# An H3 and feed-forward kernel: the convolution's f16 parts go into the signal's own place, weight factors are joined, and an output buffer is taken from a second ring

## The chip, the cores and the metric

The kernel runs on one core of a Trainium2 chip. The metric is the device time in microseconds (us) of one execution; lower is better. Engine names are those of the profile: PE (TensorE matmul), PEld (its weight load), DVE (VectorE), ACT (ScalarE), POOL (GpSimd, which here only issues adding DMAs), SP (SyncE, which issues all other DMAs).

## What is computed

With S = 2048 rows, D = 1024 channels and F = 3584 hidden features, all f32:

```python
xn = layernorm(q)
h3 = xn * (causal_conv(kv, ssm_k) + kv * ssm_D)      # kv = short_conv(k, 4 taps) * v, per channel
ff = silu(xn @ w1) @ w2
out = q + h3 + ff
```

The long convolution has 2048 taps for each of the 1024 channels. In the reference it goes by FFT.

## The kernel before, in words

**Feed-forward.** Both matrix products run in f16 with each operand split in a high and a low part, so that one logical product is three matmuls (hi*hi, hi*lo, lo*hi; lines 958 to 960 for w1, 1101 to 1103 for w2). Most of it goes by a Strassen scheme with seven products, P1 to P7, whose weight operands are called B11, T2, T3, B21, B22, T1 and T4. `factors_w1` (line 762) builds them from each pair of w1 columns on DVE (sums) and ACT plus DVE (`split`: ACT writes the high part, DVE the low one). They live in the ring `wo` (six tiles of two halves) and are also stored to DRAM (`ws`) and loaded again for the second half of the rows. Before the change T1 is a difference in a tile of its own (`t1`), split by itself, and T4 is another.

A unit is one set of seven products into PSUM banks `ff`. `evacuate` (first product) and `evacuate2` (line 1185, second product) copy banks out. In `evacuate2` the values of P6 and P5 go to `a` and `d`, P1+P2 and P3 are taken by `copied`; all of these are halves of the ring `hf` (three tiles, six halves), and each is then added to `out` by a DMA that POOL issues. In the last unit only, `copied` may take a half of the ring `ht` (two tiles, four halves) instead, and the old output that `a` needs is loaded to an `ht` half. PE may start P3 of a unit when ACT has read P5 out of the bank that they share (line 1167).

**Convolution.** It runs in 8 groups of 128 channels beside the feed-forward. For a group: `gate` (line 1468) squares the filter `kf` on ACT for its scale, makes kv in `acc` from `kin` (one ACT copy and three DVE multiply-adds for each half b of the rows) and multiplies by v in quarters. `signal_parts` (line 1519) splits `acc` by t in f16 parts: group 0 is transposed by PE first; for the others the parts go to `cm` and are transposed by DMA into tiles of the rings `hi` and `lo` (two tiles each), one tile holding signal and filter for one t. `stage1` (line 1553) multiplies them with a constant DFT matrix; `to_spec`, `forward`, `product` and `inverse` (DVE butterflies on the tile `spec`, in place) follow, then `result_parts`, `stage1_inv` and `gated`, which writes or adds to `out`. The rings `hi` and `lo` also serve as place for the quarters of v and for the outputs of the squares.

**Order.** Nothing is ordered by hand. Generators yield operations with a modelled duration and a bias, and at build time a planner (`Order.run`, line 262) picks the next one by modelled start time less bias. Each engine then runs its instructions in that order, and each DMA queue issues in that order, with semaphores between engines. Where a generator yields `ring.ready`, that is a question to the planner; the wait on the chip is on the last readers of the buffer that it got. An edit that changes a duration or a buffer can so change the order of everything planned after it.

Of the kernel before, what the change touches and what calls it, by code (L numbers as in the profile page):

```python
# [20 lines left out]
P = 128  # L21
# [40 lines left out]
FACTORS = (("B11",), ("T2", "T3"), ("B21", "B22"), ("T1",), ("T4",))  # L62
# [238 lines left out]
def h3_ffn_kernel(ctx, tc, x, kp, vs, fs, shift, dskip, w1, w2, cfwd, cinv, out):  # L301
# [132 lines left out]
    t1_r = Ring(order, rawa, "t1", 1)  # L434
# [326 lines left out]

    def factors_w1():
        for n, (kind, i) in enumerate(pairs):
# [421 lines left out]
    def evacuate2(u, one, made, seen):  # L1185

        last = u == len(tiles2) - 1

        def copied(src, tok, to):
            yield lambda: hfs.ready() or last and hts.ready()  # L1190
            o, otok = (hts if last and hts.ready() else hfs).tile([P, W])
# [22 lines left out]
        yield ws_r.ready  # L1214
        d, dt = ws_r.tile([P, W])
# [193 lines left out]
    TO = (1, 3, 0, 2)  # L1409

    def convolution(floor):
# [5 lines left out]
        def ring(name, bufs, pool=ra):  # L1417
            return Ring(order, pool, name, bufs)

        kin_r, kf_r, acc_r, hi_r, lo_r = (ring(*a) for a in (  # L1420
            ("kin", 1), ("kf", 1), ("acc", 1), ("hi", 2), ("lo", 2)))
# [5 lines left out]
        kins, kfs, accs, scs, sss, part, ipart, xgs, tmps, vals = ({} for _ in range(10))  # L1427
# [15 lines left out]
        def loads():  # L1443
            for g in range(NG):
                for b in range(2):
                    yield kin_r.ready
                    kins[g, b] = kin, _ = kin_r.tile([P, T2 + HALO, P])
                    yield L(kin, kp[g, b])
                    flag["kin", g, b].set()
                    if b == 0:  # L1450
                        yield kf_r.ready
                        kfs[g] = kf, _ = kf_r.tile([P, 2, T2, P], uses=4)
                        yield L(kf, fs[g])
                        yield G(kf[0:1, 0, 0, :], dskip[g:g + 1, :])
                        flag["kf", g].set()

        def load_v():

            for g in range(NG):
                yield flag["acc", g]  # L1460
                for b in range(2):
                    for q in range(2):
                        yield lambda: hi_r.ready() or lo_r.ready()
                        vals[g, b, q] = v, _ = (hi_r if hi_r.ready() else lo_r).tile([P, TQ, P])
                        yield L(v, vs[g, b][:, q * TQ:(q + 1) * TQ])
                        flag["v", g, b, q].set()

        def gate():

            for g in range(NG):  # L1470
# [6 lines left out]
                yield acc_r.ready  # L1477
                accs[g] = acc, _ = acc_r.tile([P, 2, T2, P])
# [6 lines left out]
                flag["acc", g].set()  # L1485
                tap = [taps[:, g, j:j + 1] for j in range(TAPS)]
                for b in range(2):
# [19 lines left out]
                yield from norm_on_two(py_r, ss[:, 0:6], (4, 2), scales, [flag["scales", g]], 4.0)  # L1507
# [3 lines left out]
        def parts_tile(hr, lr, shape=(P, 2, 2, 2, P)):  # L1511
# [7 lines left out]
        def signal_parts():  # L1519

            for g in range(NG):
                yield flag["scales", g]
                acc, atok = accs[g]
                kf, ktok = kfs[g]
                sc, _ = scs[g]
                for t in TO:
                    if g < BY_DMA:
# [8 lines left out]
                        (hi, htok), (lo, ltok) = part[g, t] = yield from parts_tile(hi_r, lo_r)  # L1536
                        flag["part", g, t].n = 2
                        add(split(hi[:, 0], lo[:, 0], px, sc[:, 0:1], (ptok, flag["part", g, t])), CB)
                        add(split(hi[:, 1], lo[:, 1], kf[:, :, t::4, :], sc[:, 1:2], (ktok, flag["part", g, t])), CB)
# [4 lines left out]
                    (hi, htok), (lo, ltok) = part[g, t] = yield from parts_tile(hi_r, lo_r)  # L1544
                    flag["part", g, t].n = 3
                    add(split(hi[:, 1], lo[:, 1], kf[:, :, t::4, :], sc[:, 1:2], (ktok, flag["part", g, t])), CB)
# [4 lines left out]
                atok.set()  # L1551

        def stage1():

            for g in range(NG):
# [3 lines left out]
                tmps[g] = tmp, _ = tmp_r.tile([P, 2, 2, 2, 2 * P])  # L1559
                for t in TO:  # L1560
                    yield flag["part", g, t]
                    (hi, htok), (lo, ltok) = part.pop((g, t))
                    two = []
                    for i in range(2):
                        for c in range(2):
                            if i == 0:
# [3 lines left out]
                                diff = (tmp[:, :, t // 2] if t % 2 else sp[:, :, 4 + t])[:, :, c]  # L1570
                                add(to_spec(g, t, sp[:, :, t, c, :], diff, *two[c], tok), CB)
# [4 lines left out]
                            def mm():  # L1576
# [3 lines left out]
                                h, l = hi[:, :, :, i], lo[:, :, :, i]  # L1580
# [3 lines left out]
                            yield T(mm, ps, [hi, lo], 0.65, m=3.0 if g > 0 and t == TO[0] else 1.0)  # L1584
                            (made if i else two[c][3]).set()
                    htok.set()
                    ltok.set()
# [17 lines left out]
        def forward(g):  # L1605
# [3 lines left out]
            def C(a, n=1, step=1):  # L1609
                t, a = (tmp, a - 8) if a >= 8 else (sp, a)  # L1610
                return t[:, :, a:a + (n - 1) * step + 1:step, :, :]

            def R(a):
                return C(a)[:, :, 0, 0, :]

            def I(a):
                return C(a)[:, :, 0, 1, :]

            def R2(a, step):
                return C(a, 2, step)[:, :, :, 0, :]  # L1620

            def I2(a, step):
                return C(a, 2, step)[:, :, :, 1, :]

            yield flag["spec", g, 1]
            yield v_tt(R2(5, 2), R2(8, 1), I2(8, 1), ADD)
            yield v_tt(I2(5, 2), I2(8, 1), R2(8, 1), SUB)
# [3 lines left out]
            yield v_tt(C(5, 2, 2), C(0, 2), C(2, 2), SUB)  # L1631
            yield v_tt(C(2, 2), C(0, 2), C(2, 2), ADD)
# [57 lines left out]
        def inverse(g):  # L1690


            def C(a, n=1, step=1):
                h, a = a // 8, a % 8
                return sp[:, h, a:a + (n - 1) * step + 1:step, :, :]

            def R(a):
                return C(a)[:, 0, 0, :]

            def I(a):  # L1700
                return C(a)[:, 0, 1, :]

            yield v_tt(C(8, 4, 2), C(0, 4, 2), C(1, 4, 2), ADD)
# [219 lines left out]
```

## Time and profile before

| | |
|---|---|
| median of 3 runs | 1249.17 us (1248.23 to 1249.23) |
| the profiled execution | 1247.09 us, span of its instructions 1245.0 us |
| granted TensorE clock | 1.00 |
| busy PE / DVE / ACT / POOL | 1232.0 / 1118.5 / 788.4 / 83.6 us |
| DMA | 279.84 MB, mean 225 GB/s |

The profile's times are microseconds from the first instruction. Busy time of an engine is the time in which at least one of its instructions was in flight; a releaser is what ended an idle stretch.

### The profile page before, as it was taken

How to read it: one execution, taken by the hardware profiler on the slowest of the kernel's cores; microseconds unless marked ns; L12 is line 12 of the kernel's file. 1: busy time of each engine (PE TensorE's matmuls, PEld its weight loads, DVE VectorE, ACT ScalarE, POOL GpSimd, SP SyncE). 2: the span in 40 equal slices, each digit the busy share in tenths (PEclk: the TensorE clock that was granted, in tenths of full speed). 3: DMA queues.
4: the chain of work that ended last, by engine and by line, in shares of the span. 5: the costliest groups of instructions: out<-in, count | busy, mean ns of one | idle time of the engine just before them, and what ended most of it. 6: DMA issues, size and time to landing. Idle time of an engine off the chain costs nothing. (4 is left out here: it accounts for less than half of the span.)

```text
span 1245.0 us, 17285 instructions
## 1 busy us (share of the span) xinstructions
PE 1232.0 (99%) x6092; PEld 601.9 (48%) x6092; DVE 1118.5 (90%) x1360; ACT 788.4 (63%) x1431; POOL 83.6 (7%) x93
## 2 busy tenths in 40 slices
PE   9999999999999999999999999999999999999997
PEld 8544444444444544444444544544544444454453
DVE  7999996996999789999999799899999889997981
ACT  7778888876688878669563823753453464554252
POOL 0000000000000000000000000000120030123223
PEclk9999999999999999999999999999999999999999
DMA  9376998879799899859984665579496498978757
GB/s 368 102 263 233 321 302 296 287 233 200 227 327 286 247 294 338 225 168 281 354 304 131 172 214 135 168 263 258 106 225 178 117 195 237 256 142 154 157 121 103
DMA packets 272807, 279.84 MB, mean 225 GB/s; under 512 B 73808, under 2 KB 192848, under 8 KB 271440
## 3 DMA queue, kind: packets, MB, share of 16 engines
q1 hardware_dynamic: 256992, 262.22, 68.2%
q0 software_dynamic: 15728, 16.52, 10.0%
q8 instruction: 47, 0.77, 0.2%
q14 instruction: 40, 0.33, 0.1%
HBM read 175.66 MB, written 88.34 MB: 212 GB/s over the span
## 5 line engine op out<-in xcount | busy, mean ns | idle before, releaser
L1101 PE MATMUL ff<-x,wo 128*128 128x512 f16 x868 | 328.1, 378 | 2.8 <-ACT hf L360 2.2
L1103 PE MATMUL ff<-x,wo 128*128 128x512 f16 x868 | 328.1, 378 | 0.0
L1102 PE MATMUL ff<-x,wo 128*128 128x512 f16 x868 | 328.1, 378 | 0.0
L958 PE MATMUL ff<-x,wo 128*128 128x512 f16 (+1 forms) x808 | 302.8, 375 | 1.3 <-DVE hf L349 0.9
L960 PE MATMUL ff<-x,wo 128*128 128x512 f16 (+1 forms) x808 | 302.8, 375 | 0.0
L959 PE MATMUL ff<-x,wo 128*128 128x512 f16 (+1 forms) x808 | 302.8, 375 | 0.0
L349 DVE TENSOR_TENSOR spec<-spec 128x512 f32<-128x512 f32 (+2 forms) x256 | 261.5, 1052 | 2.1
L1102 PEld LDWEIGHTS <-wo 128*128 128x128 f16 x868 | 84.9, 98 | 101.9 <-issue 3.3
L1103 PEld LDWEIGHTS <-wo 128*128 128x128 f16 x868 | 84.9, 98 | 101.6
L1101 PEld LDWEIGHTS <-wo 128*128 128x128 f16 x868 | 85.8, 99 | 98.8
L960 PEld LDWEIGHTS <-wo 128*128 128x128 f16 x808 | 79.0, 98 | 92.1
L958 PEld LDWEIGHTS <-wo 128*128 128x128 f16 x808 | 80.4, 100 | 87.9
L959 PEld LDWEIGHTS <-wo 128*128 128x128 f16 x808 | 79.0, 98 | 89.8 <-issue 1.9
L349 DVE TENSOR_TENSOR tmp<-spec 128x2048 f32<-128x2048 f32 (+1 forms) x48 | 92.7, 1933 | 0.9
L352 DVE SCALAR_TENSOR_TENSOR ht<-hf,wsc,ht 128x1024 f16<-128x1024 f32 (+1 forms) x56 | 67.3, 1203 | 7.0 <-ACT ht L360 5.3
L360 ACT ACTIVATE ht<-hf,wsc 128x1024 f16<-128x1024 f32 (+1 forms) x56 | 60.8, 1085 | 8.5 <-DMA hs<-ht 3.5
L352 DVE SCALAR_TENSOR_TENSOR wo<-raw,wsc,wo 128x512 f16<-128x512 f32 (+1 forms) x56 | 56.5, 1013 | 7.3 <-ACT wo L360 6.9
L360 ACT ACTIVATE spec<-spec 128x1024 bf16<-128x1024 f32 x32 | 33.7, 1054 | 45.6 <-DVE spec L349 45.6
L352 DVE SCALAR_TENSOR_TENSOR acc<-kin,taps,acc 128x1024 f32<-128x1024 f32 x48 | 61.4, 1279 | 0.6 <-ACT acc L360 0.5
L349 DVE TENSOR_TENSOR spec<-tmp 128x512 f32<-128x512 f32 (+1 forms) x80 | 60.9, 793 | 0.9
L346 POOL DMA_DIRECT2D kf<-in_dskip x8 | 7.4, 922 | 801.8 <-DMA kf<-in_fs 327.2
L346 POOL DMA_DIRECT2D out<-hf x45 | 40.7, 911 | 298.5 <-ACT hf L360 201.8
(193 smaller groups left out, 1798.7 us busy)
## 6 DMA issues: line engine op xcount, KB each, us to landing
wo<-hs SPq DMA_DIRECT2D x160, 256.0 KB, 3.5
hs<-ht SPq DMA_DIRECT2D x80, 256.0 KB, 4.3
raw<-in_w SPq DMA_DIRECT2D x28, 512.0 KB, 5.8
wraw<-in_w SPq DMA_DIRECT2D x24, 512.0 KB, 5.8
w2n<-in_w SPq DMA_DIRECT2D x24, 512.0 KB, 5.9
out<-hf POOLq DMA_DIRECT2D x45, 256.0 KB, 4.3
kin<-in_kp SPq DMA_DIRECT2D x16, 704.0 KB, 5.1
xt<-in_x SPq DMA_DIRECT2D x16, 512.0 KB, 7.4
```

Of the source, the lines that this page charges most:

```text
L346: return Op("POOL", 1.1, 3.0, lambda: nc.gpsimd.dma_start(o, i, accum_op=ADD), [i], [o], m, 2.3 * n)
L349: return V(lambda: nc.vector.tensor_tensor(o, a, b, op=op), o, [a, b], **k)
L352: return V(lambda: nc.vector.scalar_tensor_tensor(o, a, s, b, op0=op0, op1=op1), o, [a, b] + ([] if isinstance(s, float) else [s]), **k)
L360: nc.scalar.activation(o, i, func, scale=scale, **kw)
L958: nc.tensor.matmul(o, w[:, 0, k], xf[:, :, k, 0], start=first and k == 0, stop=False, **kw)
L959: nc.tensor.matmul(o, w[:, 0, k], xf[:, :, k, 1], start=False, stop=False, **kw)
L960: nc.tensor.matmul(o, w[:, 1, k], xf[:, :, k, 0], start=False, stop=last and k == KH - 1, **kw)
L1101: nc.tensor.matmul(po, hx[:, n, 0, :], wc[:, n, 0, :], start=first and n == 0, stop=False, **kw)
L1102: nc.tensor.matmul(po, hx[:, n, 0, :], wc[:, n, 1, :], start=False, stop=False, **kw)
L1103: nc.tensor.matmul(po, hx[:, n, 1, :], wc[:, n, 0, :], start=False, stop=last and n == 3, **kw)
```

## The change

Three groups of edits. **w1 factors:** T4 and T1 become one double factor: `B21|B22 - T2`, with T2 read twice by a step of 0, and one split of 1024 elements a partition for both; the tile `t1` goes, and the two are stored and loaded together. **Convolution:** `acc` and a second half of the same size become one tile `sig`; v is loaded whole for each b to the second half and multiplied in one product; the filter's f16 parts are then written to that second half in one split over the whole `kf`, and the signal's f16 parts go back to the place of `acc`, also by the transposing DMAs; `hi` and `lo` go. A group's `gate` and its loads of v now wait until `stage1` of the group before has read both. `stage1` waits for all of the filter's parts once. The butterflies get another slot order in `spec` (`AT`), by which more of them can be joined: 4 scaled additions become 2 in `forward`, and `inverse` has 13 instead of 16 instructions over the same elements. **Last unit:** `d` in `evacuate2` may take a half of `ht`, as `copied` already may.

The parts of the diff that carry this:

```diff
-FACTORS = (("B11",), ("T2", "T3"), ("B21", "B22"), ("T1",), ("T4",))
+FACTORS = (("B11",), ("T2", "T3"), ("B21", "B22"), ("T4", "T1"))
...
             yield from part(("B11",), b[0, 0])
-            yield t1_r.ready
-            t1, t1k = t1_r.tile([P, KH, P])
-            yield v_tt(t1, b[0, 1], b[0, 0], SUB)
             yield v_tt(b[0, 1], b[1, 1], b[0, 1], SUB)
             yield v_tt(b[0, 0], b[0, 1], b[0, 0], ADD)
             yield from part(("T2", "T3"), hv[0])
             yield from part(("B21", "B22"), hv[1])
-            yield from part(("T1",), t1)
-            t1k.set()
-            yield v_tt(b[1, 0], b[1, 0], b[0, 0], SUB)
+            two = hv[1].rearrange("p k (f w) -> p k f w", f=2)
+            yield v_tt(two, two, again(b[0, 0]), SUB)
             toks[0].set()
-            yield from part(("T4",), b[1, 0])
+            yield from part(("T4", "T1"), hv[1])
...
+        def place():
+            yield lambda: hfs.ready() or last and hts.ready()
+            return (hts if last and hts.ready() else hfs).tile([P, W])
...
-        yield ws_r.ready
-        d, dt = ws_r.tile([P, W])
+        d, dt = yield from place()
         yield made["P5"]
         yield a_act(d, two, AF.Copy, invc2[:, 0:1])
...
+    AT = (0, 2, 3, 1, 4, 6, 5, 7)
...
+        sig = ra.tile([P, 2, 2, T2, P], F32, name="sig")
+        acc = sig[:, 0]
+        acc16 = acc.bitcast(F16)
+        kparts = sig[:, 1].bitcast(F16).rearrange("p b t w -> p b (t w)").rearrange("p b (q t w) -> p b q t w", q=2, t=T2)
...
+        def signal(t2, q):
+            return pair(acc16[:, :, t2, q * P:(q + 1) * P], kparts[:, :, q, t2, :])
...
             for g in range(NG):
-                yield flag["acc", g]
+                if g > 0:
+                    yield flag["stage1", g - 1]
                 for b in range(2):
-                    for q in range(2):
-                        yield lambda: hi_r.ready() or lo_r.ready()
-                        vals[g, b, q] = v, _ = (hi_r if hi_r.ready() else lo_r).tile([P, TQ, P])
-                        yield L(v, vs[g, b][:, q * TQ:(q + 1) * TQ])
-                        flag["v", g, b, q].set()
+                    yield L(sig[:, 1, b], vs[g, b])
+                    flag["v", g, b].set()
...
+                if g > 0:
+                    yield flag["stage1", g - 1]
                 for a in range(2):
-                    yield hi_r.ready
-                    j, tok = hi_r.tile([P, T2, P], BF16)
-                    yield a_act(j, kf[:, a], AF.Square, total=ss[:, 4 + a:5 + a])
-                    tok.set()
+                    j = acc[:, a].bitcast(BF16)[:, 0:TQ].rearrange("p t w -> p (t w)")
+                    yield a_act(j, kf[:, a].rearrange("p t w -> p (t w)"), AF.Square, total=ss[:, 2 + a:3 + a])
...
-                    for q in range(2):
-                        yield flag["v", g, b, q]
-                        v, tok = vals.pop((g, b, q))
-                        o = acc[:, b, q * TQ:(q + 1) * TQ]
-                        yield v_tt(o, o, v, MUL)
-                        yield a_act(v, o, AF.Square, total=ss[:, 2 * b + q:2 * b + q + 1])
-                        tok.set()
+                    yield flag["v", g, b]
+                    v = sig[:, 1, b]
+                    yield v_tt(o, o, v, MUL)
+                    yield a_act(v, o, AF.Square, total=ss[:, b:b + 1])
...
+                whole = [kparts[:, :, q].rearrange("p b t w -> p b (t w)") for q in range(2)]
+                add(split(*whole, kf.rearrange("p b t w -> p b (t w)"), sc[:, 1:2], (ktok, flag["kparts", g])), CB)
                 for t in TO:
+                    there = acc16.rearrange("p b (i t) w -> p (b i) t w", i=2)[:, :, t]
+                    two = [there[:, :, q * P:(q + 1) * P] for q in range(2)]
...
-                    add(split(hi[:, 1], lo[:, 1], kf[:, :, t::4, :], sc[:, 1:2], (ktok, flag["part", g, t])), CB)
-                    for q, o in enumerate((hi, lo)):
-                        yield X(o[:, 0].rearrange("p b i w -> p (b i) w"), cm[:, q].rearrange("p b i w -> p (b i w)"))
+                    flag["part", g, t].n = 2
+                    for q, o in enumerate(two):
+                        yield X(o, cm[:, q].rearrange("p b i w -> p (b i w)"))
...
+                yield flag["kparts", g]
                 for t in TO:
                     yield flag["part", g, t]
-                    (hi, htok), (lo, ltok) = part.pop((g, t))
...
-                                h, l = hi[:, :, :, i], lo[:, :, :, i]
+                                h, l = (signal(t + 4 * i, q) for q in range(2))
...
+                flag["stage1", g].set()
...
-            for o, s, t, r in ((4, 8, 5, -RT), (5, 8, 5, RT), (6, 9, 7, -RT), (7, 9, 7, RT)):
-                flat = [C(a)[:, :, 0].rearrange("p s c w -> p s (c w)") for a in (o, s, t)]
-                yield v_stt(flat[0], flat[1], r, flat[2], MUL, ADD)
+            yield v_stt(long(sp[:, :, 4:6]), long(tmp), -RT, long(sp[:, :, 6:8]), MUL, ADD)
+            yield v_stt(long(sp[:, :, 6:8]), long(tmp), RT, long(sp[:, :, 6:8]), MUL, ADD)
```

More of the change, by code (lines that the diff above doesn't have):

```diff
@@ L1187, in evacuate2 @@
         last = u == len(tiles2) - 1
+        def place():
+            yield lambda: hfs.ready() or last and hts.ready()
+            return (hts if last and hts.ready() else hfs).tile([P, W])
         def copied(src, tok, to):
-            yield lambda: hfs.ready() or last and hts.ready()
-            o, otok = (hts if last and hts.ready() else hfs).tile([P, W])
+            o, otok = yield from place()
             yield a_act(o, src, AF.Copy, invc2[:, 0:1])
@@ L1426, in convolution @@
         ctxs["nm"] = py_r
-        kins, kfs, accs, scs, sss, part, ipart, xgs, tmps, vals = ({} for _ in range(10))
+        kins, kfs, scs, sss, ipart, xgs, tmps = ({} for _ in range(7))
         more = {}
@@ L1690, in inverse, with C @@
         def inverse(g):
[L1693 to L1695 removed]
+            def C(a, b=None):
+                one = sp[:, a // 8, AT[a % 8]].rearrange("p c w -> p (c w)")
+                return one if b is None else pair(one, C(b))
             def R(a):
[L1698 removed]
+                return C(a)[:, 0:2 * P]
             def I(a):
[L1701 removed]
@@ L1739, in result_parts @@
                     (hi, htok), (lo, ltok) = ipart[g, t] = yield from parts_tile(more["zh"], more["zl"], (P, 2, 2 * 2 * P))
-                    yield from split(hi, lo, sp[:, 1, t::4].rearrange("p i c w -> p i (c w)"), sc[:, 4:5],
+                    two = pair(sp[:, 1, AT[t]], sp[:, 1, AT[4 + t]]).rearrange("p i c w -> p i (c w)")
+                    yield from split(hi, lo, two, sc[:, 4:5],
                                      (flag["taken", g, t], flag["ipart", g, t]))
```

93 lines of the change are left out of this document (40 added, 53 removed).

## The prediction

> **What bounds the kernel now.** I read the page first, then one long window of the table of windows, then PE's timeline at each of its gaps.
>
> ```profile
> span 1245.0 us, 17285 instructions
> PE 1232.0 (99%) x6092; PEld 601.9 (48%) x6092; DVE 1118.5 (90%) x1360; ACT 788.4 (63%) x1431; POOL 83.6 (7%) x93
> 15.72:1232.30 1216.58, 1212.71 (x5956) 585.17 (x5954) 1105.92 (x1324) 776.94 (x1406) 80.26 (x84) 1.00 0.79 225
> ```
>
> PE is busy for 1232.0 of 1245.0 us. The third line is the stretch from the first feed-forward matmul to the gap near the end: PE is busy for 1212.71 of 1216.58 us, so only 3.87 us are idle there. Is a busy PE also full? Consecutive 128x512 matmuls tell:
>
> ```profile
> 1230.87 0.38 PE L1101 MATMUL ff<-x,wo 128*128 128x512 f16 x1
> 1231.09 0.38 PE L1102 MATMUL ff<-x,wo 128*128 128x512 f16 x1
> 1231.31 0.38 PE L1103 MATMUL ff<-x,wo 128*128 128x512 f16 x1
> ...
> 1231.95 0.38 PE L1103 MATMUL ff<-x,wo 128*128 128x512 f16 x1
> ```
>
> They last 0.38 us each but start 0.216 us apart (1.08 us from the first to the fourth shown, five steps with the two left out), one hiding behind the other. How many of that shape there are:
>
> ```profile
> L1101 PE MATMUL ff<-x,wo 128*128 128x512 f16 x860 | 325.9, 379 | 2.2 <-ACT hf L360 2.2
> L958 PE MATMUL ff<-x,wo 128*128 128x512 f16 x776 | 294.0, 379 | 1.3 <-DVE hf L349 0.9 <-ACT x L360 0.5
> L1581 PE MATMUL ps<-hi,cfw 128*128 128x512 f16 x108 | 40.9, 379 | 0.6 <-ACT tmp L360 0.6
> ```
>
> Three lines each of the first two kinds, and stage 1 with 384 in the source (8 groups, 4 values of t, 2 x 2 x 3; 108 of the 128 of a line go to `ps`, the others to `ff`): 3 x 860 + 3 x 776 + 384 = 5,292, times 0.216 = 1,143 us. The rest of 1232 is taken by shapes of half that width, transposes and warm-up. So PE is at its pace nearly throughout. The Trainium skill ("Perfetto Trace Analysis", Identifying the Most-Contended Engine) says that matmul busy time is a bad measure of headroom and names the share of weight loads instead; that share is 48% here and by it half the time could still be won. The start times above decide otherwise: the busy time holds no hidden slack.
>
> The change leaves every matmul and its size as it is, except small sums for norms (4 columns in place of 6). So DVE, ACT and DMA can move the time only through PE's gaps. These are the ones after the start phase:
>
> ```profile
> 42.44 1.82 PE L598 MATMUL ft<-ident,xt 128*128 128x128 f32 x12 [0.34 <-DVE x L352]
> 45.43 0.63 PE L598 MATMUL ft<-ident,xt 128*128 128x128 f32 x4 [1.17 <-DVE x L352]
> 204.01 0.38 PE L958 MATMUL ff<-x,wo 128*128 128x512 f16 x1 [0.46 <-ACT x L360]
> 323.88 0.38 PE L958 MATMUL ff<-x,wo 128*128 128x512 f16 x1 [0.87 <-DVE hf L349]
> 430.52 0.38 PE L1581 MATMUL ps<-hi,cfw 128*128 128x512 f16 x1 [0.60 <-ACT tmp L360]
> 782.88 0.27 PE L1773 MATMUL py<-zl,civ 128*128 128x256 f16 x1 [0.41 <-DVE zl L352]
> 1234.56 0.38 PE L1101 MATMUL ff<-x,wo 128*128 128x512 f16 x1 [2.23 <-ACT hf L360]
> ```
>
> The first six sum to 3.85 us, which is the idle time of the long window. The last, 2.23 us, is the only large one, and it stands where nothing can make it up.
>
> **The gap at 1232.3 us.** ACT, POOL and SP there:
>
> ```profile
> 1216.77 3.34 POOL L346 DMA_DIRECT2D out<-ht  x3 [0.55 <-issue]
> 1217.29 0.33 SPq L336 DMA_DIRECT2D ht<-out  x1
> 1222.60 2.22 POOL L346 DMA_DIRECT2D out<-ht  x2 [2.50 <-issue]
> 1224.60 0.69 ACT L360 ACTIVATE hf<-ff,invc 128x512 f32<-128x512 f32 x1 [4.49 <-PE ff L1103]
> 1227.61 1.78 POOL L346 DMA_DIRECT2D out<-hf  x2 [2.79 <-issue]
> 1228.24 5.48 DMA out<-hf
> 1233.83 0.69 ACT L360 ACTIVATE hf<-ff,invc 128x512 f32<-128x512 f32 x1 [8.54 <-DMA out<-hf]
> ```
>
> This is the last unit: P6 is copied at 1224.60 into `a`, P5 at 1233.83 into `d`. A product is 12 matmuls, 2.59 us, so P7 and P5 follow to about 1229.8 and P2 to 1232.3. `d` could thus have been copied at 1229.8. But its `hf` half was still being added to `out` by a DMA that POOL issued at 1228.24 (behind the convolution's last `out<-ht` additions) and that landed at 1233.72. P3 waits for `d`, hence 2.23 us of idle PE.
>
> **The change part by part.** (1) *Last unit.* `d` may now be a half of `ht`. The load of the old output takes one half, at 1217.29; a second half of the same tile is picked first. It last held a result of the convolution whose addition was issued in the `out<-ht` batches of 1216.77 or, at worst, 1222.60 to 1224.82. Landing in the 5.48 us of the row above, that is about 1225 or, at worst, 1230.3; with the copy's 0.69 us `d` is read by 1231.0, before P2 ends at 1232.3. So the whole 2.23 us goes: what is late next is P2 itself, which is PE's own work. The rest of the tail moves as one: P3, two halves of P4, one DVE addition and the last stores. Gain 2.2 us; bounds 0 (no half of `ht` is free for the planner) and 2.23.
>
> (2) *w1 factors.* Fourteen pairs, with rows
>
> ```profile
> L352 DVE SCALAR_TENSOR_TENSOR wo<-raw,wsc,wo 128x1024 f16<-128x1024 f32 x28 | 35.7, 1278 | 4.3 <-ACT wo L360 4.1
> L360 ACT ACTIVATE wo<-raw,wsc 128x1024 f16<-128x1024 f32 x28 | 31.9, 1140 | 2.9 <-DVE raw L349 2.9
> L352 DVE SCALAR_TENSOR_TENSOR wo<-raw,wsc,wo 128x512 f16<-128x512 f32 x28 | 20.7, 747 | 3.0 <-ACT wo L360 2.8
> L360 ACT ACTIVATE wo<-raw,wsc 128x512 f16<-128x512 f32 x28 | 19.8, 714 | 7.3 <-DVE raw L349 2.8 <-DVE pow L495 2.3 <-issue 1.2
> L349 DVE TENSOR_TENSOR spec<-spec 128x1024 f32<-128x1024 f32 x104 | 125.1, 1219 | 0.6
> L349 DVE TENSOR_TENSOR spec<-spec 128x512 f32<-128x512 f32 x128 | 83.4, 686 | 1.0
> L349 DVE TENSOR_TENSOR spec<-spec 128x2048 f32<-128x2048 f32 x24 | 54.9, 2288 | 0.5
> ```
>
> DVE per pair: four sums of 512 (4 x 0.686) and two splits (2 x 0.747) become two sums of 512, one of 1024 and one split (1.372 + 1.219 + 1.278): 4.24 to 3.87, less 0.37; ACT 2 x 0.714 to 1.140, less 0.29. Over 14 pairs 5.1 and 4.0 us. T1 comes some 2 to 3 us later than now, but P5, its product, is the fifth of its unit, over 10 us (4 x 2.59) after the unit's start, and no row of PE waiting for `wo` exists. On PE: 0, between -0.4 and +0.4 for a shifted place in the queue.
>
> (3) *Convolution, per group on DVE.* `forward`: four scaled sums of 1024 (1.22 each, taken as the sum's 1.219) to two of 2048: 4.88 to 4.58. `inverse`: 2.288 + 7 x 1.219 + 8 x 0.686 = 16.31 to 2.288 + 10 x 1.219 + 2 x 0.686 = 15.85. Product with v: 4 x 0.686 to 2 x 1.219, less 0.31. Filter's low parts: four pieces of 512 (2.99) to one of 2048; from 747 and 1278 ns, 1.04 ns an element, so 2.34 us, an estimate. Sum: less 1.7 us a group, 13.6 us in all. ACT: the filter's high parts 2.86 to about 1.99 (same reckoning from 714 and 1140), and two fewer squares. Together with (2) DVE sheds 18.7 of 1118.5 us. Nothing of it lies on PE's path: convolution work must only reach PE before its feed-forward work runs out, and it does:
>
> ```profile
> L1772 PE MATMUL py<-zh,civ x112: 271/273/273, 414.8 to 1214.4; 128*128 128x256 f16 x112
> ```
>
> Its last matmuls are at 1214.4, PE's last at 1240.7. On PE: 0.
>
> (4) *Parts ready ahead.* Now two of four parts of a group are made within `stage1`, as `hi` and `lo` hold two each. There ACT waits for the transposing DMA and PE for ACT:
>
> ```profile
> 427.04 0.72 ACT L360 ACTIVATE cm<-acc,csc 128x512 f16<-128x512 f32 x1 [1.57 <-DMA lo<-cm]
> ```
>
> This is 3.5 us ahead of the gap at 430.52. With all four parts made before `stage1`, that wait is elsewhere and I count the 0.60 us as gone; bounds 0 and 0.60.
>
> (5) *What is added.* The filter's split is one ACT piece of 2.0 and one DVE piece of 2.3 us. PE leaves 2.59 us (one product) between the end of P1 and its need of the copied bank, and the copy takes
>
> ```profile
> L360 ACT ACTIVATE ff<-ff 128x512 f32<-128x512 f32 x34 | 19.8, 582 | 19.2 <-PE ff L960 12.2 <-PE ff L1103 6.5
> ```
>
> 0.58: a piece started just before loses at most 2.0 + 0.58 - 2.59, about 0, and up to 0.3 with the hand-overs between engines: 8 pieces, 0 to 2.4 us. I take 0.2, near the lower end, as pieces of 2.29 us stand on DVE today and few end in a gap. The other four gaps after 200 us or before (0.46, 0.87, 0.41, and 1.51 of the transposes, planned before any edited step) I leave as they are.
>
> **Sum.** -2.2 - 0.6 + 0.2 = -2.6 us, 1247.09 to 1244.5 for the profiled execution. The median before, 1249.17, lies 2.1 above that execution; on its scale the sum gives 1246.5.
>
> **The rivals.** *ACT held at a gate (slower).* `gate` starts with ACT squares of `kf` that now write into the place of `acc`, so that ACT, in order, stands until `stage1` of the group before has been through PE. Behind it wait the copies of PE's banks, and PE for them. The trace shows this for another wait:
>
> ```profile
> 202.24 1.06 ACT L360 ACTIVATE hi<-kf 128x1024 bf16<-128x1024 f32 x1 [2.79 <-DMA kf<-in_dskip]
> 203.29 0.67 ACT L360 ACTIVATE x<-ff,wsc 128x512 f32<-128x512 f32 x1
> ```
>
> 2.79 us of ACT wait gave PE's 0.46 at 204.01. It decides where ACT stands longer than about 1.7 us (2.59 - 0.58 - 0.3) before a copy. With a loss of 0.9 us (the 0.87 gap) at each of seven gates: -2.2 + 6.3 = +4.1, 1253.3. Against it: the planner knows PE's order, and PE is seldom late, while a DMA's landing is what it misjudges; and `kf`, free earlier, has landed by then. The same price would come of loads of v standing in SP's queue ahead of the feed-forward's `wo` loads.
>
> *Slower transposes (same).* Their target was one run of 512 f16 in a partition and becomes four runs of 128 in the place of `acc`. No row of before shows that form. `cm` has one tile, so that ACT waits at the next split until both transposes have landed:
>
> ```profile
> ACT cm L360 <- DMA lo<-cm: 19.9, 7, 4.8
> DMA to landing us min/median/max: 2.4/2.8/6.4
> ```
>
> Seven such waits cost PE 0.60 us once. If all land at the slow end, 6.4 us, ACT stands longer at each group; with 0.6 us of PE for each of seven groups the time is -2.2 + 4.2 = +2.0, 1251.2. For it speaks only the new form; against it that a slow landing today mostly costs PE nothing. The Trainium skill ("DMA: Bandwidth & Descriptors", Latency and other measured facts) gives transposes with a non-contiguous middle dimension some 30% less bandwidth, which speaks for it; no row here tests it. Chance 0.05, within the same-case.
>
> *Gain eaten (same; the change to `d` does not do what it says).* `d` finds its `ht` half late, or the order remade by the planner brings as many short gaps as it removes. With the tail's 2.23 won and 1 us of new gaps: 1248; with no gain at all 1249.2.
>
> *All gaps go (faster).* -2.23 - 0.46 - 0.87 - 0.60 - 0.41 = -4.6: 1244.6, the floor, since nothing of PE's own work goes.
>
> **How the numbers follow.** A change of 0.2%, 2.5 us, is about what a measurement can tell from none. The forecast of -2.6 stands just beyond it. Forecast with the floor case: 0.48, that is 1244.6 to 1246.7. Eaten or slower transposes: 0.26 + 0.05 = 0.31, 1246.7 to 1251.7. Slower: 0.21, 1251.7 and up. The range reaches from 1243.8 (the floor less the 0.9 us by which one run before lies under the median) to 1251.5, leaving out most of the slower case.
>
> **What would show it.** In the changed profile: `ht<-ff,invc` copies in the last unit are three, with no wait of PE near its end; busy DVE near 1100 and ACT under 780; last `py` matmuls earlier than 1214; no `cm` wait inside `stage1`; PE busy near 1232. I am wrong if PE's rows show waits for ACT after `acc<-kf` squares, if the last unit still waits for an `out` addition, or if PE's pace between matmuls differs from 0.216.

## The result and the profile after

| | before | after |
|---|---|---|
| median, 7 runs each | 1249.21 us | 1253.67 us (1252.18 to 1256.06) |
| ratio | | 1.0038, 95% interval 1.0028 to 1.0048 |
| the profiled execution, its span | 1247.09, 1245.0 | 1252.18, 1250.1 |

The change makes the kernel slower by 0.38%; the forecast was 1246.5 and the range ended at 1251.5. The page of the changed kernel:

```profile
span 1250.1 us, 17015 instructions
PE 1235.8 (99%) x6092; PEld 602.9 (48%) x6092; DVE 1108.4 (89%) x1252; ACT 779.5 (62%) x1361; POOL 83.3 (7%) x93
```

DVE and ACT are less busy, as meant, and PE is *more* busy with the same 6092 matmuls. These are PE's idle stretches after the start phase, as its timeline marks them, with the matmuls on either side of the cluster (1087.45 and 1101.25):

```profile
1074.51 0.38 PE L1100 MATMUL ff<-x,wo 128*128 128x512 f16 x1 [0.54 <-ACT ff L360]
1087.45 0.38 PE L1100 MATMUL ff<-x,wo 128*128 128x512 f16 x1
1088.45 0.38 PE L1101 MATMUL ff<-x,wo 128*128 128x512 f16 x1 [0.61 <-DVE x L352]
1089.81 0.38 PE L1100 MATMUL ff<-x,wo 128*128 128x512 f16 x1 [0.77 <-ACT x L360]
1090.91 0.58 PE L1101 MATMUL ff<-x,wo 128*128 128x512 f16 x1 [0.73 <-DVE x L352]
1093.78 0.58 PE L1101 MATMUL ff<-x,wo 128*128 128x512 f16 x1 [1.43 <-DVE x L352]
1095.14 0.59 PE L1100 MATMUL ff<-x,wo 128*128 128x512 f16 x1 [0.35 <-ACT x L360]
1097.51 0.59 PE L1101 MATMUL ff<-x,wo 128*128 128x512 f16 x1 [1.78 <-DVE x L352]
1101.25 0.38 PE L1101 MATMUL ff<-x,wo 128*128 128x512 f16 x1
1245.29 0.27 PE L1100 MATMUL ff<-x,wo 128*128 128x256 f16 x1 [0.58 <-DVE hf L352]
```

All five gaps of before between 204 and 1235 us are gone; the last unit has no wait but the 0.58 of its halves, which before had too (0.57). In their place stands one stall, at the first unit of the second product. PE waits there for `x`: the f16 factor of T4 for w2 (built in `norms_w2`, line 1304: four times a sum `raw - hold` on DVE, then ACT's high part and DVE's low part), wanted by P4. Its six waits sum to 5.67 us. The windows show the second half of the loss (column after POOL: the granted clock):

```profile
1085.00:1090.00 5.00, 3.62 (x17) 1.46 (x15) 5.00 (x9) 2.18 (x4) 0.86 (x1) 1.00 0.99 221
1090.00:1095.00 5.00, 2.63 (x6) 0.66 (x5) 5.00 (x7) 2.62 (x5) 0.86 (x1) 0.60 0.84 165
1095.00:1100.00 5.00, 3.08 (x7) 0.94 (x7) 4.93 (x6) 1.24 (x3) 0.00 (x0) 0.50 0.03 5
1100.00:1105.00 5.00, 5.00 (x23) 2.27 (x22) 4.96 (x5) 0.00 (x0) 0.86 (x1) 0.88 0.44 82
```

The clock falls to 0.50 and matmuls last 0.58 to 0.63. From 1087.45 to 1101.25 PE made 19 steps in 13.80 us where its pace of 0.216 would have taken 4.10: 9.70 us are lost. With 0.54 at 1074.51, less the 2.23 and the 2.34 (0.46 + 0.87 + 0.60 + 0.41) of before: +5.67, against +5.1 of span. So, to within 0.6 us, the loss is this one place.

Why is T4 late? Some rows of DVE's timeline in both kernels, before first:

```profile
1085.71 1.28 DVE L349 TENSOR_TENSOR x<-w2n,x 128x512 f32<-128x512 f32 x2
1087.57 0.68 DVE L349 TENSOR_TENSOR x<-wraw,x 128x512 f32<-128x512 f32 x1
1089.50 0.68 DVE L349 TENSOR_TENSOR x<-wraw,x 128x512 f32<-128x512 f32 x1
1090.76 1.28 DVE L349 TENSOR_TENSOR spec<-tmp 128x512 f32<-128x512 f32 x2
1091.97 0.74 DVE L352 SCALAR_TENSOR_TENSOR x<-x,tau,x 128x512 f16<-128x512 f32 x1
```

```profile
1085.12 0.68 DVE L349 TENSOR_TENSOR x<-wraw,x 128x512 f32<-128x512 f32 x1
1088.31 0.69 DVE L349 TENSOR_TENSOR x<-wraw,x 128x512 f32<-128x512 f32 x1
1088.91 0.69 DVE L349 TENSOR_TENSOR x<-w2n,x 128x512 f32<-128x512 f32 x1
1090.78 2.29 DVE L349 TENSOR_TENSOR tmp<-spec 128x2048 f32<-128x2048 f32 x1
1093.64 0.69 DVE L349 TENSOR_TENSOR x<-w2n,x 128x512 f32<-128x512 f32 x1
1094.24 1.29 DVE L349 TENSOR_TENSOR spec<-spec 128x512 f32<-128x512 f32 x2
1095.57 1.23 DVE L349 TENSOR_TENSOR tmp<-tmp,spec 128x1024 f32<-128x1024 f32 x1
1096.71 0.74 DVE L352 SCALAR_TENSOR_TENSOR x<-x,tau,x 128x512 f16<-128x512 f32 x1
```

Before, T4's sums start at 1085.71, one pair of convolution pieces (`spec`, 1.28 us) stands between the first sum and the last split, and T4 is done at 1092.71, with no wait of PE. After, the first sum is even earlier, but 5.5 us of convolution pieces (2.29 + 1.29 + 1.23, and one of 0.69 among the rows left out) stand between the third sum and the last split, and 1.4 us more (two of the rows left out) between the first and the second; T4 is done at 1097.45. DVE has no idle time there: the two streams share it and the planner took the other one first. It was not the loads: the raw weights of T4's four sums had landed 5.3 to 7.4 us before the sums that read them (the last was issued at 1082.77 and landed 3.5 us later; its sum starts at 1093.64).

PE also comes earlier. These two rows of its timeline in the kernel before are P4's first matmul and the one that reads the last piece of T4:

```profile
1090.62 0.38 PE L1101 MATMUL ff<-x,wo 128*128 128x512 f16 x1
1092.78 0.38 PE L1102 MATMUL ff<-x,wo 128*128 128x512 f16 x1
```

That piece was finished at 1092.71, so T4 was in time by 0.07 us. In the changed kernel P4 starts at 1087.45, 3.2 us earlier: 1.80 us less idle time lies ahead of it (2.34 less 0.54), and six matmuls of `stage1` (1.30 us) that stood ahead of it now come behind. At full pace the last piece would have been read ten steps later, at 1089.61. It was 7.8 us late, 4.7 because T4 was finished later and 3.2 because PE came earlier, less the 0.07.

**Theory A** was thus the order on DVE (with the halved clock behind it). Its rivals: **B**, the joined w1 factors; **C**, ACT standing at `cm` behind the transposing DMAs; **D**, a clock that falls by itself; **E**, biases that would help any such kernel; **F**, butterflies that are slow by their new strides. For C speaks this, 15 us ahead of the stall (ACT's timeline, then DVE's; the bracket is the idle time before and what ended it):

```profile
1070.93 0.72 ACT L360 ACTIVATE cm<-sig,csc 128x512 f16<-128x512 f32 x1 [3.31 <-DMA sig<-cm]
```

```profile
1071.69 0.75 DVE L352 SCALAR_TENSOR_TENSOR cm<-sig,csc,cm 128x512 f16<-128x512 f32 x1 [0.93 <-ACT cm L360]
1074.01 0.75 DVE L352 SCALAR_TENSOR_TENSOR x<-wraw,tau,x 128x512 f16<-128x512 f32 x1 [1.57 <-ACT x L360]
```

### The profile page after: what moved, and what is told of

Same layout as the page of the kernel before. It is cut to its first block, busy times and chain, and to the rows that moved or that the text cites. A ratio compares the mean times of both kernels' runs of the same rounds, so it can differ in the third digit from the quotient of the medians.

```text
span 1250.1 us, 17015 instructions
## 1 busy us (share of the span) xinstructions
PE 1235.8 (99%) x6092; PEld 602.9 (48%) x6092; DVE 1108.4 (89%) x1252; ACT 779.5 (62%) x1361; POOL 83.3 (7%) x93
## 3 DMA queue, kind: packets, MB, share of 16 engines
q0 software_dynamic: 15728, 16.52, 10.2%
## 4 chain that ended last, share of the span: by engine, by line
PE 95%; DVE 3%; ACT 1%; DMA 1%; issue 0%; SPq 0%; ACTq 0%
PE ff L1101 14%; PE ff L1102 14%; PE ff L1100 14%; PE ff L957 14%; PE ff L958 14%; PE ff L959 14%; PE ps L1579 2%; PE ps L1580 2%; PE ps L1581 2%; PE py L1768 1%; PE py L1769 1%; PE py L1767 1%; PE ft L597 1%; DVE x L352 1%; DVE spec L349 1%
## 5 line engine op out<-in xcount | busy, mean ns | idle before, releaser
L349 DVE TENSOR_TENSOR spec<-spec 128x1024 f32<-128x1024 f32 (+2 forms) x232 | 259.6, 1146 | 2.0
L352 DVE SCALAR_TENSOR_TENSOR wo<-raw,wsc,wo 128x1024 f16<-128x1024 f32 (+1 forms) x56 | 64.0, 1146 | 8.3 <-ACT wo L360 8.1
L352 DVE SCALAR_TENSOR_TENSOR sig<-kin,taps,sig 128x1024 f32<-128x1024 f32 x48 | 61.5, 1280 | 11.2 <-ACT sig L360 11.1
L360 ACT ACTIVATE wo<-raw,wsc 128x1024 f16<-128x1024 f32 (+1 forms) x56 | 58.0, 1036 | 12.4 <-DVE raw L349 7.3
```

The lines of the kernel that those rows point to most:

```text
L349: return V(lambda: nc.vector.tensor_tensor(o, a, b, op=op), o, [a, b], **k)
L352: return V(lambda: nc.vector.scalar_tensor_tensor(o, a, s, b, op0=op0, op1=op1), o, [a, b] + ([] if isinstance(s, float) else [s]), **k)
L360: nc.scalar.activation(o, i, func, scale=scale, **kw)
```

## The experiments

"T4 waits" are PE's waits for `x` at this place, in the profiled execution; ratios are to the kernel before, with 95% intervals. Executions of one kernel lie some us apart (of before, 1246.70 to 1252.40), so a profiled execution shows where the waits are, and the medians price a change.

| kernel | T4 waits, us | median, us | ratio |
|---|---|---|---|
| after | 5.67 | 1253.67 | 1.0038 (1.0028 to 1.0048) |
| e1 after, w2 first | 0 | 1245.56 | 0.9961 (0.9949 to 0.9973) |
| e2 before, w2 first | 0 | 1252.68 | 1.0029 (1.0019 to 1.0040) |
| e3 after, old butterflies | 0.21 | 1246.98 | 0.9980 (0.9969 to 0.9991) |
| e4 after, old signal place | 0 | 1249.73 | 1.0007 (0.9997 to 1.0016) |
| e5 before, last unit | 0 | 1245.41 | 0.9963 (0.9951 to 0.9976) |
| e6 before, signal place | 0.68 | 1252.15 | 1.0027 (1.0016 to 1.0039) |
| e7 before, butterflies | 0.22 | 1247.65 | 0.9985 (0.9976 to 0.9993) |
| e8 after, old w1 factors | 4.99 | 1259.61 | 1.0082 (1.0069 to 1.0096) |
| e9 after, second cm place | 7.40 | 1261.80 | 1.0099 (1.0086 to 1.0112) |
| e10 before, w1 factors | 0 | 1247.30 | 0.9993 (0.9981 to 1.0006) |
| e11 before, last unit and butterflies | 0.21 | 1247.55 | 0.9980 (0.9971 to 0.9989) |
| e12 e3, w2 first | 0 | 1248.49 | 0.9992 (0.9984 to 1.0001) |
| e13 after, no last transposes | 5.28 | 1250.50 | 1.0014 (1.0005 to 1.0023) |
| e14 before, w2 later | (below) | 1269.23 | 1.0160 (1.0146 to 1.0174) |
| e15 after, splits first | 4.38 | 1254.08 | 1.0038 (1.0025 to 1.0051) |

**e1 and e2: only the planner's bias.**

```diff
-            for gen, bias in (..., (norms_w2(), 0.03)):
+            for gen, bias in (..., (norms_w2(), 0.1)):
...
-                add(split(..., src, tau2[:, i:i + 1], toks), 0.05)
+                add(split(..., src, tau2[:, i:i + 1], toks), 0.12)
```

> The changed kernel with two biases raised and nothing else: the w2 factors' generator from 0.03 to 0.10 and the splits of its last five factors from 0.05 to 0.12, so that the planner takes them ahead of the convolution's gate and parts. Theory A (the f16 factor of T4 of w2 is late for the first unit of the second product, because the convolution's work of the last group now lies in the same stretch; PE idles 5.67 us there and then runs at a granted clock of 0.5 to 0.9, 9.70 us in all): the stall from 1087 to 1101 goes, PE's waits for x near 1090 sum to under 1 us, the clock stays at 1.00, and the time is 1253.7 - 9.7 = 1244.0, at most 1246. Rival C (ACT stands at cm behind the transposing DMAs, 21.9 us in nine waits, and the splits on ACT come late for that): those waits are in the landing of the DMAs and stay, so at least half of the stall stays: 1249 to 1254. Rival D (the clock falls by itself, since the denser DVE work draws more): the clock falls below 0.9 again without a wait ahead of it: about 1248 (the idle time goes, some 4 us of slow clock stay).

> The kernel before with the same two biases raised. Theory A: there P4 took T4 of w2 without a wait, so nothing is to be won: 1249.2, within 1 us. Rival E (these biases are simply better and would give any such kernel 5 us, so that e1 says nothing of the change): 1244 to 1246.

e1's timeline of PE has these gaps left after the start phase, beside two of 0.55 and 0.27 for `zl` and the 0.57 at the end:

```profile
441.65 0.38 PE L1579 MATMUL ps<-sig,cfw 128*128 128x512 f16 x1 [2.04 <-DVE spec L349]
1088.22 0.38 PE L1100 MATMUL ff<-x,wo 128*128 128x512 f16 x1 [0.81 <-ACT hf L360]
```

The stall is gone, the clock stays at 1.00 in every window from 1085 to 1110, and the median falls by 8.1 us to within A's bounds (the profiled span by 5.9). ACT still waits at `cm`, 24.3 us in ten waits against 21.9 in nine: those waits alone don't make the stall. D falls too. e2 misses its expectation by 3.5 us on the other side: the same biases cost the kernel before a new wait of 2.48 us for ACT's copy of `ff` at 1080.41, with a halved clock behind it, and one of 1.23 us at 894. So the bias is no gain by itself (against E); it mends the order that this change brings.

**e3, e4, e8: the changed kernel less one group of edits.** e3 takes back `forward`, `inverse`, `AT` and `result_parts`; e4 `sig`, `load_v`, `gate`, `signal_parts`; e8 the w1 factors.

> The changed kernel with the butterflies, the slot order in spec and the result's parts of before; the signal's place, the joined w1 factors and the last unit stay changed. Theory A says that it is the moment at which the convolution's work of the last group meets the w2 factors that decides. Without the joined butterflies DVE has some 0.1 us more for each of 5 fewer instructions a group, the chain of the last group comes 2 to 4 us later against PE, and less of it is ahead of T4: the stall is shorter, 0 to 4 us in place of 9.7, and the time 1244 to 1248. If the signal's place alone makes the stall (A in its plain form): 1253 to 1255. If the butterflies' new strides were slow by themselves (rival F): DVE's busy time falls below that of the changed kernel though it issues more instructions.

> The changed kernel with the convolution's parts as before: acc, hi and lo in tiles of their own, v in quarters, two of four parts made within stage 1; the butterflies, the w1 factors and the last unit stay changed. Theory A: the parts are again made in the holes that DVE and ACT have within stage 1, so the w2 factors are in time: no slow clock near 1090, and of the time before remains the 2.2 us of the last unit: 1247, and up to 1250 if the gaps at 204, 324, 430 and 783 come back with others. Rival B (the joined w1 factors make the loss, through later weights): 1252 to 1255.

> The changed kernel with T4 and T1 of w1 apart again, as before. Theory A: the stall near 1090 stays, since the w1 factors are long done there: 1252 to 1256, granted clock under 0.9 between 1090 and 1105. Rival B (the joined w1 factors shift the convolution against PE so that it meets the w2 factors): the stall goes, 1244 to 1247.

In this change the stall needs both the signal's place and the joined butterflies: without either the T4 waits are 0.21 us or nothing. Without the joined w1 factors it stays (4.99 us of waits) and the time is 6 us worse, with other waits of 3.58 us for `hf` at 504 and 1.86 at 603 for a load of `wo`; so B falls. F as well: in e3 DVE is busy for 1110.3 us in 1292 instructions, after for 1108.4 in 1252.

**e5, e6, e7, e10, e11: one or two groups of edits on the kernel before.**

> The kernel before with the edit of the last unit alone (d may take a half of ht). Step (1) of the prediction: the 2.23 us gap near 1232 goes and nothing ahead of it changes: 1249.2 - 2.2 = 1247.0, the other gaps as before (0.46, 0.87, 0.60, 0.41). Rival (gain eaten): d finds no half or the gap turns up again at the next step, 1249.

> The kernel before with only the signal's and the filter's parts moved (tile sig, v whole, filter split in one). Theory A in its plain form (this edit alone puts the last group's work ahead of T4 of w2): the stall near 1090 with a granted clock under 0.9, 1254 to 1256. Theory A with the meeting in time deciding (e3, which has this edit and no stall, took 1247.0 with the last unit's 2.2 won): 1249, within 2 us, gaps near 1090 under 2 us, and the 2.2 us near the end still there.

> The kernel before with only the joined butterflies and the slot order. DVE's busy time less by 5 to 8 us (8 groups, 2 + 3 instructions fewer over the same elements; the prediction's rows would give 6.1). By the prediction nothing of it on PE: 1249.2, within 1 us, if the order of the rest holds; by theory A no stall near 1090, as the parts are still made within stage 1.

> The kernel before with T4 and T1 of w1 joined and nothing else. By the prediction's step (2): 0 on PE, 1249.3 within 1 us, 2.23 us near the end still there. If the parts added up, e4 (1249.7, with the last unit and the butterflies changed too) less e5 (-3.9) and e7 (-1.7) would leave +6: 1255; and the changed kernel less e8 would leave -6: 1243. That these two differ by 12 says that the parts don't add up; a result far from 1249 says that a shifted order in the w1 stretch costs more than the 0.4 us allowed.

> The kernel before with the edit of the last unit and the butterflies, neither the signal's place nor the w1 factors. If the two add up: 1249.3 - 3.9 - 1.7 = 1243.7. If the butterflies alone had won only by bringing the last convolution outputs ahead of d, they win the same 2.2 us, and the time is that of e5, 1245 to 1246. By theory A no stall near 1090.

In e5 `d` (the second of these rows of ACT's timeline) goes to a half of `ht` right after P5, and PE has no wait there:

```profile
1229.70 0.69 ACT L360 ACTIVATE hf<-ff,invc 128x512 f32<-128x512 f32 x1 [4.49 <-PE ff L1103]
1234.88 0.69 ACT L360 ACTIVATE ht<-ff,invc 128x512 f32<-128x512 f32 x1 [4.49 <-PE ff L1103]
```

It won 3.9 us by the medians (3.0 to 6.1 by the interval), more than the 2.2 expected; its profiled execution was its slowest (1249.2), with gaps of 1.59 and 1.99 us elsewhere and 3.4 us of halved clock behind the second, so the surplus could not be placed. e6 has no stall and is slower all the same, by other waits (1.75 and 1.61 us for DVE at 594 and 900, 1.23 for ACT at 884): the plain form of A falls, and so does "within 2 us of 1249". e7 and e10 lose the 2.23 us gap near the end *without* the edit meant for it, and both lie below the 1249 expected of them. In e7 the order brings the convolution's last additions earlier (the last one is issued at 1217.81, before the change at 1223.32). In e10 they are later (1228.46) and ACT still waits for an addition before it copies P5, but it does so at 1232.20 while PE, 1.9 us later at this unit, is still at P2; e10 pays with waits of 2.60 us at 1083 and 1.33 at 522. e11 missed both its expectations and is no faster than e7: the two win the same gap, and e11 has 2.18 at 1081. The parts do not add up: the four alone come to -3.9 + 2.8 - 1.7 - 2.3 = -5.1 us (the last of them not clear of noise), the whole is +4.5.

**e9 and e13: ACT's wait for the transposes.** e9 gives every second pair of the last group's parts a second place (`kin`); e13 issues no transposes for the last group, whose `stage1` reads the filter's parts instead, so that the group's result is left out:

```diff
-                        yield X(o, cm[:, q]. ...)
+                        x = X(o, cm[:, q]. ...)
+                        if g == NG - 1:
+                            x.emit = lambda: None
+                        yield x
```

> The changed kernel in which the last group's second and fourth pair of cm parts are written to the place of kin, which is free by then, so that ACT need not wait there for the transposes of the part before. Rival C (ACT's wait of 3.31 us at cm near 1070 is the cause: behind it DVE idles 0.93 + 1.57 us, and T4 is late by that): the wait goes, DVE's idle 2.5 us go with it, T4's last split comes some 2.5 us earlier, the stall falls from 9.7 to 3 to 6 us: 1247 to 1250. Theory A (it is the order of DVE's work; time that DVE gains goes to the convolution's next piece): PE's waits for x stay over 4 us and the clock falls: 1251 to 1256.

> The changed kernel, in the same order on ACT, DVE and PE, without the eight transposing DMAs of the last group; its stage 1 reads the filter's parts in place of the signal's, so the last group's result is left out, by which no time but that of the waits changes. Rival C (ACT's stand at cm makes T4 late): the waits of 2.75 and 3.31 us go, DVE's 2.5 us of idle time near 1070 go, T4's last split comes 2.5 us earlier, and the stall falls from 9.7 us by that and by the slow clock that goes with it, to 3 to 5 us: 1247 to 1249. Theory A (the order on DVE is the cause, ACT's wait adds little): the stall stays over 7 us, 1251 to 1254.

e9 went wrong in both theories' terms (+8 us). ACT waited at the new place as well (its timeline in e9):

```profile
1058.91 0.72 ACT L360 ACTIVATE kin<-sig,csc 128x512 f16<-128x512 f32 x1 [6.05 <-DMA sig<-cm]
1067.85 0.72 ACT L360 ACTIVATE cm<-sig,csc 128x512 f16<-128x512 f32 x1 [4.79 <-DMA sig<-kin]
```

The second row waits for transposes out of `kin` though `cm` had been free since 1058.9: which leaves `sig` itself, read by the split and written by the transposes of the t before. That is concluded by elimination; no run separates it. A second `cm` did not let the two overlap; planned as if it did, ACT stood longer and PE lost 5.36 us at 1077.95. e13 prices the wait with nothing reordered. ACT and DVE run through near 1070, T4's last split starts at 1094.15 instead of 1096.71, 2.56 us earlier, and PE's gaps in its timeline are

```profile
1088.36 0.38 PE L1101 MATMUL ff<-x,wo 128*128 128x512 f16 x1 [0.47 <-DVE x L352]
1091.22 0.38 PE L1101 MATMUL ff<-x,wo 128*128 128x512 f16 x1 [2.06 <-DVE x L352]
1092.58 0.38 PE L1100 MATMUL ff<-x,wo 128*128 128x512 f16 x1 [0.76 <-ACT x L360]
1094.95 0.59 PE L1101 MATMUL ff<-x,wo 128*128 128x512 f16 x1 [1.99 <-DVE x L352]
```

From P4's first matmul to the return of the full clock (1086.86 to 1100.33, 23 steps) that is 13.47 less 4.97: 8.5 us lost instead of 9.7. So C is real but small in the stall, 1.2 of the 9.7 us, and the stall that is left is what A expected (over 7). The median is 3.2 us lower, 1250.5, between what the two expected, and the profiled span 1.9; 0.54 of that is the gap at 1074.51, which e13 does not have.

**e14: the converse in the kernel before. e15: one of the two biases.**

```diff
-            for gen, bias in (..., (norms_w2(), 0.03)):
+            for gen, bias in (..., (norms_w2(), 0.02)):
```

> The kernel before with the bias of the w2 factors' generator lowered from 0.03 to 0.02 and nothing else, the converse of e1. Theory A: before stood at the edge, its T4 split ended at 1092.7 with PE taking it at once; with the factors behind the convolution's work PE waits for w2's factors between 1080 and 1120 with a granted clock under 0.9, and the time is 1255 to 1275. If before had slack there (the stall then needs something that only the change brings): 1249, within 2 us.

> The changed kernel with only the splits of the last five w2 factors raised (0.05 to 0.12), the generator that issues their loads and DVE sums left at 0.03. Theory A in its closer form (the sums raw - hold on DVE are what the convolution's pieces go ahead of): the stall stays: 1251 to 1256. If the splits behind ACT are what is late: the stall goes as in e1, 1244 to 1247.

A hundredth of bias makes the tuned kernel 20 us slower, with PE waiting (three of the rows of its timeline)

```profile
1087.56 0.59 PE L1101 MATMUL ff<-x,wo 128*128 128x512 f16 x1 [5.41 <-ACT x L360]
1089.11 0.59 PE L1102 MATMUL ff<-x,wo 128*128 128x512 f16 x1 [0.96 <-DVE x L352]
1128.85 0.38 PE L1102 MATMUL ff<-x,wo 128*128 128x512 f16 x1 [1.34 <-DVE x L352]
```

for w2's factors, and the convolution behind it as well (`py`, `ps`). The planner's order decides here too, but by another road than T4's sums, which start only at 1125.64: ACT stood for a scale of the convolution, and the splits of the factors stood behind it (a row of ACT's timeline in e14):

```profile
1084.70 0.30 ACT L480 ACTIVATE csc<-pow 128x1 f32<-128x1 f32 x2 [4.12 <-DVE pow L497]
```

e15 leaves the stall (4.38 us, and another wait of 2.96 at 1078): raising the splits alone does not do it. What it left at 0.03 are the sums; the loads have a generator and a bias of their own (`load_w2`, 0.05), which neither e1 nor e15 changes. The sums raised alone were not run.

**e12** put both on e3.

> e3 (the changed kernel with the butterflies of before) with the two biases of e1. Theory A: e3 had 0.21 us of T4 waits left, so the biases win next to nothing there: 1246 to 1247.5; a candidate for the fastest if the 1.47 us wait at 1081 goes with the new order: 1245.

It missed by 1 us: the T4 waits went, and the 1.47 us at 1081 became 0.49, but a wait for `zl` grew from 1.24 to 1.68 and new ones of 0.68, 0.64 and 0.37 came. The fastest versions are e1 and e5, whose intervals overlap; both beat before and after.

## Why the prediction was wrong

**The step that failed** is in (3): "Nothing of it lies on PE's path: convolution work must only reach PE before its feed-forward work runs out". The reason given was the last `py` at 1214.4 against PE's end. But DVE serves a third customer, the w2 factors, which have a due time of their own, PE's start of P4. The prediction read who waits for DVE only through PE's present gaps. A factor that arrives just in time shows no gap, and T4 of before was one, by 0.07 us. In the changed kernel its last piece was finished 4.7 us later and PE wanted it 3.2 us earlier: the stall cost 9.7 us where the step had put 0. What the prediction called the floor ("all gaps go", 1244.6) took every gap as won for good; with 0.07 us to spare at P4, time saved ahead of it is kept only if T4 comes earlier too. The median of e1, 1245.6, came near the floor; its profiled execution has T4 done at 1092.02, in time, and 3.7 us of other gaps after 200 us (the final 0.57 left out).

**The rival's price.** "Gain eaten" spoke of an order remade by the planner and allowed 1 us for new gaps; the price was 9.7. Two things were missing in it: that T4's sums are four in a row, so that every piece put among them delays P4 again, and that waits in close succession can halve the clock, which here turned 5.7 us of idle time into 9.7. The rival "ACT held at a gate" named 1253.3, nearly the measured time, by luck: in the changed kernel ACT has no idle time before any of the 16 squares of `kf`, and none of the signs that the prediction listed was a wait for w2's factors.

**(1), the last unit**, was right in mechanism: three `ht` copies, no wait, shown by e5, the run with this edit alone, and in the changed kernel. That the same gap can vanish by order (e7, e10) was not seen.

**(2), w1 factors**: "0 on PE, between -0.4 and +0.4" holds alone only as a balance: the time is the same within the measurement (e10, 0.9981 to 1.0006), but gaps of 2.60 and 1.33 us came and the one of 2.23 went. Taking the edit out of the changed kernel costs 6 us.

**(3), the sizes.** DVE shed 10.1 us, not 18.7; alone, w1 3.8 (5.1 predicted; e10 1114.7), the butterflies 3.6 (6.1; e7 1114.9), the signal's place 5.1 (7.5; e6 1113.4). The term mis-sized is the price of an instruction: the row's mean counts time in which the next one already runs. Four neighbours of DVE's timeline in e3:

```profile
1083.50 0.68 DVE L349 TENSOR_TENSOR spec<-tmp 128x512 f32<-128x512 f32 x1
1084.10 0.68 DVE L349 TENSOR_TENSOR x<-wraw,x 128x512 f32<-128x512 f32 x1
1084.70 0.68 DVE L349 TENSOR_TENSOR spec<-tmp 128x512 f32<-128x512 f32 x1
1085.31 0.68 DVE L349 TENSOR_TENSOR x<-w2n,x 128x512 f32<-128x512 f32 x1
```

They start 0.60 apart. A 1024 piece is followed after 1.14 (1095.57 to 1096.71 above), so joining two saves 0.06 us, not 2 x 0.686 - 1.219 = 0.15. PE's pace had been read from starts; DVE's was not. ACT shed 8.9 us and ended at 779.5, as said.

**(4)** held for the 0.60 gap. "No `cm` wait inside `stage1`" nearly held (two of the nine, 0.37 us at 673 and 1.70 at 981, come after a group's first six matmuls there), but "that wait is elsewhere" was left unpriced, and elsewhere was the stretch of the w2 factors (e13: 1.2 us of the stall). The transposes land later than before, at a median of 3.6 us against 2.8 (the view of the tile `cm`, after):

```profile
DMA to landing us min/median/max: 2.4/3.6/7.4
```

That this comes from the new form of the target, as the rival had it, is not shown: in e7 and e11, which keep the old form, the median is 3.8.

**(5)**: the pieces last 1.99 and 2.35 us as estimated, and no PE wait stands behind one. The last `py`, forecast "earlier than 1214", is at 1221.8.

**What stays open**: how the signal's place and the butterflies bring about this order together, when each alone does not. That the convolution's chain runs later is not enough: its seventh group's product starts at 1049.4 before, 1058.7 after, and at 1060.1 in e1, which has no stall. Nor is the surplus of e5 explained.

## What to carry to other kernels

Before an engine is called off the critical path, list every consumer that it feeds and when each wants its data; one that is served just in time shows no wait and may have no slack, and an edit that moves work can make a greedy planner serve it late. Test such a change together with a small shift of the planner's weights, since the order was worth more here (8.1 us in e1, 20 in e14) than the edit itself. Price joined instructions by start to start, not by the row's mean.

## What the runs showed of the hardware

The granted clock does not need a long pause to halve. In e2 one gap of 2.48 us did it (clock by the windows; the gap ends at 1080.41):

```profile
1081.00:1082.00 1.00, 1.00 (x5) 0.40 (x3) 1.00 (x3) 0.00 (x1) 0.14 (x1) 0.63 0.97 307
1083.00:1084.00 1.00, 1.00 (x4) 0.45 (x3) 1.00 (x2) 0.72 (x1) 0.00 (x0) 0.50 1.53 109
1085.00:1086.00 1.00, 1.00 (x7) 0.41 (x6) 1.00 (x2) 0.57 (x1) 0.00 (x0) 1.00 1.15 179
```

In e5 one of 1.99 us was enough (its gap in PE's timeline, then a window):

```profile
896.13 0.27 PE L1775 MATMUL py<-zl,civ 128*128 128x256 f16 x1 [1.99 <-DVE zl L352]
898.00:899.00 1.00, 1.00 (x3) 0.30 (x2) 0.00 (x0) 1.00 (x2) 0.00 (x0) 0.50 0.00 0
```

The clock took about 3.4 us to come back in both, as after the 3.58 us gap of e8; the longer stretches at 0.50 are about two, three or four times that (6.8 us in e13 and e14, 10.2 in the changed kernel, 13.7 in e9). In the changed kernel three gaps of 0.61, 0.77 and 0.73 us within 3.5 us were enough. Gaps of 2.23 (before), 2.30 (e6) and 2.60 us (e10) left the clock at 1.00. The Trainium skill ("TensorE: Matmul & The Clock Gate", Part 1: The HAM clock gate) says that a free-running window of about 3.4 us decides, which fits a threshold that varies with the moment and stretches of about that length; its condition of at least one idle window of that length does not fit, as 1.99 us sufficed and PE was not idle for a whole such window in the changed kernel either.
